# Forward substitution of two matrix sets at a time in a delta-rule attention kernel, with a separate early transpose of K

## Chip, cores and metric

The kernel runs on one core of a Trainium2 chip. The metric is device time in microseconds (us) of one execution. Engines: TensorE (PE; its weight loads are shown as PEld), VectorE (DVE), ScalarE (ACT), GpSimd (POOL) and SyncE (SP, which here only issues DMAs).

## What is computed

Inputs: q, k, v of shape (4, 8, 768, 48), beta (4, 8, 768), and the router and weights of 8 experts.

```python
k_n = k / (norm(k) + 1e-6); state = 0
for t in range(768):                       # for each of 4 x 8 heads
    y[t]  = q[t] @ state
    v_old = k_n[t] @ state
    state = state + beta[t] * outer(k_n[t], v[t] - v_old)
x = y, as 3072 tokens of 8 * 48 = 384
expert = argmax(x_n @ en.T / tau);  gate = softmax(...)[expert]
out[token] = gate * (relu(x[token] @ w1[expert]) @ w2[expert])   # 384 -> 1024 -> 384
```

All of it is in float32.

## The kernel before, in words

**Two halves.** The first half is the attention, in which each token also gets its expert. The second half (from line 1105 on) goes through the experts' token tiles of 128, some 11 us of TensorE each, with weights streamed by SP. Two expert tiles of expert 0 (`early_tile`) are already done at the end of the first half.

**Chunks, units, groups.** The sequence of 768 is cut into 12 chunks of 64 steps (`m`). A unit (`n`, 24 of them) is one chunk for two of the four batch entries, 16 heads at once; the units of one half of the batch follow each other through a state S, so two chains of units alternate. A group (`g`, 6 of them) is two chunks, or four units.

**What a unit does** (`unit`, line 626). Inside a chunk the sequential rule is a triangular system. A unit multiplies K with the state (`old`), subtracts from V (`rest`, VectorE), solves with the inverses of the two 32x32 blocks on the diagonal (`solve`, `fix`, `solve_again`, with copies out of PSUM by ScalarE between them), updates the state (`update`, `new_state` on VectorE), and adds the part from the state and the part inside the chunk to the output (`from_state`, `inside`). Then come the transposes of the output, the router's logits (`logits_out` on VectorE) and, for each four units, the routing.

**The inverses** are made ahead, a group at a time, by `prepare(g)` (line 422). K is loaded and normalised (the sums of squares, roots and the product `keys`), transposed on TensorE (`turned`, line 305) and evicted by ScalarE into `KQ`, whose other half holds q transposed. `gram_diag` makes the 32x32 Gram blocks on the diagonal: for a group 2 x 64 matmuls into one PSUM pair. A 32x32 transpose (`to_lanes`, line 546) puts them so that each of 128 partitions (lanes) holds one 32x32 matrix X. `lower` on GpSimd clears the upper part. Then VectorE substitutes column by column, lines 556 to 568: for j from 1 to 30 a product (line 561) and a subtraction (line 565) over (31 - j) * j elements. Each instruction needs the one ahead of it. That is 60 instructions a group, 360 in all. `from_lanes` (line 573) transposes back into `WT` (one buffer), and ScalarE spreads that into W (two instructions, `spread`), which all `solve` steps of the group's four units read. Some buffers (k, X, WT) lie in the space that later holds the first expert's weights.

**What sets the order.** Nothing is scheduled while the kernel runs: each engine executes its instructions in a fixed order. That order comes from `Plan` (line 29): each step is added with an engine, a cost, a due time (`key`, in units of `PERIOD` = 7.5 us) and what it reads and writes; `order` plays the steps through with these costs and always takes the ready step with the earliest due time. PSUM is four pairs of banks, which steps take and give back. So a change of a cost or of a due time can move any instruction.

SP issues the loads of k, q and v: each is cut into issues of 48 or 96 KB, 20 issues for a chunk (some of the first by other engines).

Of the kernel before, what the change touches and what calls it, by code (L numbers as in the profile page):

```python
# [11 lines left out]
ALU = mybir.AluOpType  # L12
# [4 lines left out]
C = 64  # L17
# [122 lines left out]
def kernel(  # L140
# [68 lines left out]
    def at(name, i):  # L209
        return name, i % len(rings[name])  # L210
# [9 lines left out]
    buffers("q", 2, [2, H, C])  # L220
    buffers("v", 3, [2, H, D])
    buffers("sq", 1, [2, H, D])
    buffers("K", 6, [2, H, C])
    buffers("KQ", 5, [2, NP, 2, 2 * C])
    buffers("rn", 2, [2, 2, NP, 2])
    buffers("rt", 2, [2, 2, NP, 2])
    quots = ac.tile([128, 2, 2, NP, 2], F32, name="quots")
    rings["X"], rings["WT"] = carved(2, [HC, HC], w2_flat), carved(3, [HC, HC], w2_flat)[2:]
    buffers("tmp", 2, [(HC // 2) * (HC // 2)])
    buffers("W", 2, [HC, C])  # L230
    buffers("Sx", 3, [H, C])
# [91 lines left out]

    flat_buffers("V", 3, 4 * NP * D)
    for name, n in (("S", 2), ("R", 2), ("Y", 2), ("U", 2), ("Z", 3)):
# [74 lines left out]
    def beta_refine(part):  # L400
# [4 lines left out]
    plan.add("POOL", 1.5, 0.2, -200.0, start_constants,  # L405
             writes=["ident", "half", "iotas"] + [("K", i) for i in range(6)] + [("q", i) for i in range(2)])

# [11 lines left out]
    def group_key(g):  # L419
        return 4 * g * PERIOD  # L420

    def prepare(g):
        ms = (2 * g, 2 * g + 1)
        t0 = group_key(g)
        for m in ms:
# [58 lines left out]
        for part in (slice(0, 1), slice(1, 2)) if g == 0 else (slice(0, 2),):  # L484
            xs = range(part.start, part.stop)
            those, roots_of = [at("rn", g) + (x,) for x in xs], [at("rt", g) + (x,) for x in xs]
            if g < 2:
                plan.add(*act(16 * len(xs)), t0 - 10 * PERIOD, roots_act(part), reads=those + ["half"], writes=roots_of)
            else:
                plan.add("POOL", 5.5, 0.2, t0 - 10 * PERIOD, roots(part), reads=those + ["half"], writes=roots_of)  # L490
            plan.add("DVE", 1.1 if g < 2 else 0.5, 0.2, t0 - 9.6 * PERIOD - (g == 0) * 30, scales(part), hold=g == 0,
                     reads=those, writes=roots_of + ["quots"])
            plan.add("DVE", 0.12 * len(xs), 0.2, t0 - 9.6 * PERIOD, scaled(part), hold=g == 0,
                     reads=[("sqb", 2 * g + x) for x in xs], writes=roots_of)

        def keys(m):
# [6 lines left out]

        def transposes(src, m, name):
            def step():
                turned(pair((name, m)), buf(src, m))
            return step

        def out_of_psum(m, name, cols):
            def step():  # L510
                act_copy(buf("KQ", m).rearrange("d i j y c -> d (i j y) c")[:, :, cols],
                         pair((name, m)).rearrange("d i (x c) -> d (i x) c", c=C))
            return step

        def gram_diag(m):
            def step_():
                p = pair(("diag", g))
                KQ = buf("KQ", m)
                for step in range(2 * NP):
                    for y in range(2):  # L520
                        for hf in range(2):
                            for jj in range(2):
                                n = 2 * NP - 1 - step if hf else step
                                rows = slice(jj * C, jj * C + D)
                                i, j, x = n // NP, n % NP, m % 2 * 2 * NP + n
                                r = (y ^ jj) * C + hf * HC
                                c, w = (0, C) if step < 2 * NP - 1 else (hf * HC, HC)
                                to = x * HC + c - hf * HC
                                mm(p[r:r + HC, jj, to:to + w], KQ[rows, i, j, y, hf * HC:(hf + 1) * HC], KQ[rows, i, j, y, c:c + w])
            return step_  # L530
        for m in ms:
            plan.add(*(dve(850) if m == 1 else pool(768)), t0 - 9.2 * PERIOD + (m % 2) * PERIOD, keys(m), hold=g == 0,
                     reads=[("k", m % 4, 0), ("k", m % 4, 1), at("rt", g) + (m % 2,)], writes=[at("K", m)])
            plan.add(*pe(8, 0.11), t0 - 8.6 * PERIOD + (m % 2) * PERIOD, transposes("K", m, "KT"), mode=2,
                     reads=[at("K", m), "ident"], take=("KT", m))
            plan.add(*act(1024), t0 - 8.4 * PERIOD + (m % 2) * PERIOD, out_of_psum(m, "KT", slice(0, C)),
                     reads=[("psum", ("KT", m))], writes=[at("KQ", m) + ("K",)])
        for m in ms:
            first = m % 2 == 0
            plan.add(*pe(64, 0.02), t0 - 7.2 * PERIOD, gram_diag(m), mode=1, reads=[at("KQ", m) + ("K",)],  # L540
                     writes=[("X_next", g % 2)] + ([] if first else [("psum", ("diag", g))]),
                     take=("diag", g) if first else None)
        X = buf("X", g)

        def to_lanes():
            nc.vector.transpose(X, pair(("diag", g)).rearrange("p jj (x c) -> p c jj x", c=HC))
        plan.add(*dve(1024), t0 - 6.5 * PERIOD, to_lanes, hold=g == 0, reads=[("psum", ("diag", g))],
                 writes=[at("X", g), ("X_next", g % 2)])

        def lower():  # L550
            nc.gpsimd.affine_select(out=X, in_=X, compare_op=ALU.is_ge, fill=0.0, base=-1,
                                    pattern=[[1, HC], [-1, HC]], channel_multiplier=0)
            nc.gpsimd.memset(X.rearrange("p a b -> p (a b)")[:, ::HC + 1], -1.0)
        plan.add("POOL", 1.2, 0.1, t0 - 6.4 * PERIOD, lower, writes=[at("X", g)])

        for j in range(1, HC - 1):
            rows = HC - 1 - j
            t = buf("tmp", j)[:, 0:rows * j].rearrange("p (a b) -> p a b", b=j)

            def product(j=j, rows=rows, t=t):  # L560
                nc.vector.tensor_tensor(t, X[:, j + 1:, j:j + 1].broadcast_to([128, rows, j]),  # L561
                                        X[:, j:j + 1, 0:j].broadcast_to([128, rows, j]), op=ALU.mult)

            def subtract(j=j, rows=rows, t=t):
                nc.vector.tensor_tensor(X[:, j + 1:, 0:j], X[:, j + 1:, 0:j], t, op=ALU.subtract)  # L565
            key = t0 - (6.0 - j * 4.0 / HC) * PERIOD
            plan.add("DVE", rows * j / 960 + 0.085, 0.13, key, product, reads=[at("X", g)], writes=[at("tmp", j)], hold=g == 0)
            plan.add("DVE", rows * j / 960 + 0.085, 0.13, key + 0.01, subtract, reads=[at("tmp", j)], writes=[at("X", g)], hold=g == 0)

        WT, W = buf("WT", g), buf("W", g)  # L570

        def from_lanes():
            nc.vector.transpose(WT, X)
        plan.add(*dve(1024), t0 - 1.9 * PERIOD, from_lanes, reads=[at("X", g)], writes=[at("WT", g), ("X_next", g % 2)])
        for b, name in enumerate(("nfirst", "nsecond")):
            def spread(b=b, name=name):
                act_copy(W[:, :, b * HC:(b + 1) * HC], WT.rearrange("p i x -> p x i"), K[name])
            plan.add(*act(1024, True), t0 - 1.8 * PERIOD, spread, reads=[at("WT", g), "masks"], writes=[at("W", g) + (b,)])

# [3 lines left out]
    def queries(m):  # L583
# [8 lines left out]

        def transposes():
            turned(pair(("QT", m)), buf("q", m))

        def evict():
            act_copy(buf("KQ", m).rearrange("d i j y c -> d (i j y) c")[:, :, C:],
                     pair(("QT", m)).rearrange("d i (x c) -> d (i x) c", c=C))
        plan.add(*pe(8, 0.11), t0 - 3.5 * PERIOD, transposes, mode=2, reads=[at("q", m) + (i,) for i in range(2)] + [("q", m % 2)] + ["ident"],
                 take=("QT", m))  # L600
        plan.add(*act(1024), t0 - 3.4 * PERIOD, evict, reads=[("psum", ("QT", m))], writes=[at("KQ", m) + ("Q",)])

# [406 lines left out]
    def early_tile(i, t0):  # L1009
# [47 lines left out]
        plan.add("PE", 0.4, 0.3, t0, transposes, mode=2, reads=[("xg", i), "ident"], take=("early_x", i))  # L1057
        plan.add(*act(384), t0 + 0.1, xT_out, reads=[("psum", ("early_x", i))], writes=["early_xT"])
        for f in range(NF):
            plan.add("PE", 0.7, 0.3, t0 + f, hidden(f), mode=2, reads=["early_xT", "w1_first"], take=("early_h", i, f))  # L1060
            plan.add(*act(128), t0 + f + 0.1, hidden_out(f), reads=[("psum", ("early_h", i, f))],
                     writes=[("early_hT", f)])
        for f in range(NF):
# [4 lines left out]

    prepare(0)
    constants()  # L1070
    for g in range(NG):
        for m in (2 * g, 2 * g + 1):
            queries(m)
            values(m)
        if g + 1 < NG:
            prepare(g + 1)
        if g == NG - 1:
# [218 lines left out]
```

## Time and profile before

| | us |
|---|---|
| median of 14 runs (lowest, highest) | 647.62 (643.64, 652.78) |
| the profiled execution, its time | 649.65 |
| its span in the profile | 647.9 |

| engine | busy, us | share of the span | instructions |
|---|---|---|---|
| PE | 551.6 | 85% | 9995 |
| DVE | 267.8 | 41% | 749 |
| ACT | 180.4 | 28% | 327 |
| POOL | 167.3 | 26% | 217 |

The profile also has the span in 40 slices with the busy share of each engine in tenths, and the clock that TensorE was granted (PEclk). Groups of instructions are shown as: line, engine, operation, output<-inputs, shapes, count | busy us, mean ns of one | idle time of the engine ahead of them, and whose end ended it. Rows in order of time have the start and the duration in us. Rows by stretch of time have, for each engine, the busy us and the number of instructions, then the granted clock and the DMA engines' share. A float32 matmul counts as two instructions.

### The profile page before, as it was taken

To read this page: it belongs to the slowest core of one execution; us is meant where nothing else is said; L and a number is where in the kernel's file an instruction comes from. 1 tells how busy PE (TensorE), PEld (TensorE's weight loads), DVE (VectorE), ACT (ScalarE), POOL (GpSimd) and SP (SyncE) were. 2 spreads that over 40 slices of the span, in tenths; PEclk is the share of its full clock that TensorE was granted. 3 is DMA by queue.
4 is the path that set the end of the run, shared out by engine and by line. 5 is a ranking of instruction groups with operands and counts; after the bars stand their busy time and mean duration, and the time that the engine had idled before them with its cause. 6 is when DMAs were issued, how large, how long until landed. Compare 5 with 4: busy or idle time off the path is not lost. (4 is left out here: it accounts for less than half of the span.)

```text
span 647.9 us, 22729 instructions
## 1 busy us (share of the span) xinstructions
PE 551.6 (85%) x9995; PEld 464.9 (72%) x9995; DVE 267.8 (41%) x749; ACT 180.4 (28%) x327; POOL 167.3 (26%) x217
## 2 busy tenths in 40 slices
PE   3563787778887888789997999999999999999991
PEld 3452676677776877678975787878788888878780
DVE  4898769669789687813232111111111111111100
ACT  2322625526527346354430111110101010101010
POOL 4434334254252131312221211212121212121100
PEclk9875669579879789968997999999999999999997
DMA  4444744533414221222013999999999999999500
GB/s 77 80 81 80 195 73 80 124 70 64 102 31 102 84 51 28 65 95 79 32 39 120 387 385 393 380 343 313 338 320 332 311 323 331 337 320 324 208 25 6
DMA packets 127911, 115.46 MB, mean 178 GB/s; under 512 B 83754, under 2 KB 113873, under 8 KB 127810
## 3 DMA queue, kind: packets, MB, share of 16 engines
q1 hardware_dynamic: 122242, 102.93, 51.6%
q0 software_dynamic: 4480, 10.85, 4.5%
q8 instruction: 80, 1.31, 0.8%
q10 hardware_dynamic: 1088, 0.20, 0.2%
q14 instruction: 21, 0.17, 0.1%
HBM read 102.02 MB, written 12.72 MB: 177 GB/s over the span
## 5 line engine op out<-in xcount | busy, mean ns | idle before, releaser
L1164 ACT ACTIVATE hT<-acc 128x512 f32<-128x512 f32 x52 | 31.1, 597 | 259.4 <-PE acc L1162 259.4
L1162 PEld LDWEIGHTS acc<-xTm,w 128*128 128x128 f32 x816 | 93.8, 192 | 4.5
L1162 PE MATMUL acc<-xTm,w 128*128 128x128 f32 x816 | 93.9, 275 | 0.0
L1169 PE MATMUL acc<-w,hT 128*128 128x384 f32 x272 | 90.5, 486 | 0.0
L1172 POOL DMA_INDIRECT out_dram<-y,ids x26 | 26.3, 1011 | 205.7 <-DVE y L1171 195.9
L1169 PEld LDWEIGHTS acc<-w,hT 128*128 128x128 f32 x272 | 50.4, 190 | 31.5
L565 DVE TENSOR_TENSOR w_first<-w_first,tmp 128x30 f32<-128x30 f32 (+9 forms) x180 | 69.6, 388 | 3.9
L1154 DVE COPY xTm<-acc 128x384 f32<-128x384 f32 x26 | 14.5, 558 | 134.4 <-PE acc L1153 134.4
L561 DVE TENSOR_TENSOR tmp<-w_first 128x30 f32<-128x30 f32 (+9 forms) x180 | 66.2, 370 | 4.1
L1171 DVE TENSOR_SCALAR y<-acc,xg 128x384 f32<-128x384 f32 x26 | 16.1, 618 | 125.0 <-PE acc L1169 125.0
L273 PE MATMUL psum_pair<-KQ 48*32 48x64 f32 (+2 forms) x2304 | 48.7, 271 | 18.7 <-issue 8.9
L273 PEld LDWEIGHTS psum_pair<-KQ 48*32 48x32 f32 (+1 forms) x2304 | 41.6, 137 | 24.1 <-issue 11.6
L1162 PEld LDWEIGHTS acc<-xTm,w_first 128*128 128x128 f32 x432 | 52.4, 201 | 3.2 <-DVE xTm L1154 1.0
L1162 PE MATMUL acc<-xTm,w_first 128*128 128x128 f32 x432 | 52.6, 284 | 0.8 <-DVE xTm L1154 0.8
L1169 PE MATMUL acc<-w_first,hT 128*128 128x384 f32 x144 | 47.9, 486 | 0.0
L273 PE MATMUL psum_pair<-S,KQ 48*64 48x64 f32 x1408 | 35.5, 249 | 10.3 <-issue 4.4
L273 PEld LDWEIGHTS psum_pair<-S,KQ 48*64 48x64 f32 x1408 | 30.7, 160 | 13.3 <-issue 5.9
L1169 PEld LDWEIGHTS acc<-w_first,hT 128*128 128x128 f32 x144 | 26.7, 190 | 16.7
L276 ACT ACTIVATE KQ<-psum_pair 128x1024 f32<-128x1024 f32 x24 | 24.5, 1023 | 42.8 <-PE psum_pair L309 33.7
L960 POOL DMA_INDIRECT idmap<-tokid,slots_i x24 | 24.2, 1008 | 42.6 <-DVE slots_i L936 13.2
L1137 POOL DMA_INDIRECT xg<-x_dram,ids x26 | 25.4, 975 | 37.7 <-DMA ids<-idmap 22.6
L615 POOL TENSOR_TENSOR V<-v,sqb 128x384 f32<-128x384 f32 x24 | 20.7, 866 | 49.8 <-DVE R L670 31.6
(183 smaller groups left out, 747.6 us busy)
## 6 DMA issues: line engine op xcount, KB each, us to landing
w<-in_moe_w_dram SPq DMA_DIRECT2D x34, 1536.0 KB
w_first<-in_moe_w_dram SPq DMA_DIRECT2D x16, 1536.0 KB
q<-in_q_dram SPq DMA_DIRECT2D x96, 48.0 KB
v<-in_v_dram SPq DMA_DIRECT2D x48, 96.0 KB
w_first<-in_k_dram SPq DMA_DIRECT2D x88, 48.0 KB
x_dram<-XC SPq DMA_DIRECT2D x5, 800.0 KB
idmap<-space SPq DMA_DIRECT2D x1, 2048.0 KB
w_first<-in_moe_w_dram SPq DMA_DIRECT2D x6, 256.0 KB
```

The costliest lines, as they stand in the source:

```text
L273: nc.tensor.matmul(out_, lhsT=lhsT, rhs=rhs, start=start, stop=True, skip_group_check=True)
L276: nc.scalar.activation(out_, in_, ACT.Copy, scale=scale)
L561: nc.vector.tensor_tensor(t, X[:, j + 1:, j:j + 1].broadcast_to([128, rows, j]), X[:, j:j + 1, 0:j].broadcast_to([128, rows, j]), op=ALU.mult)
L565: nc.vector.tensor_tensor(X[:, j + 1:, 0:j], X[:, j + 1:, 0:j], t, op=ALU.subtract)
L615: nc.gpsimd.tensor_tensor(buf("V", m)[:, i * 2 * NP * D:(i + 1) * 2 * NP * D].rearrange("p (jj j d) -> p jj j d", jj=2, d=D), buf("v", m)[ ...
L960: put = nc.gpsimd.indirect_dma_start(out=idmap[:, :], out_offset=bass.IndirectOffsetOnAxis(ap=slot_i[:, i:i + 1], axis=0), in_=K["tokid"][ ...
L1137: t.read = nc.gpsimd.indirect_dma_start(out=t.x, out_offset=None, in_=x_dram[:, :], in_offset=bass.IndirectOffsetOnAxis(ap=t.ids[:, 0:1], ...
L1162: nc.tensor.matmul(psH[:, i, :], lhsT=t.w1[:, j, (f + i) * 128:(f + i + 1) * 128], rhs=t.xT[:, j, :], start=(j == 0), stop=(j == KC - 1))
L1164: nc.scalar.activation(t.hT[:, f:f + 4, :], psH, ACT.Relu)
L1169: nc.tensor.matmul(psO, lhsT=t.hT[:, f, :], rhs=t.w2[:, f, :], start=(f == 0), stop=(f == NF - 1))
L1171: nc.vector.tensor_scalar_mul(y, psO, t.x[:, Dm:Dm + 1])
L1172: nc.gpsimd.indirect_dma_start(out=out[:, :], out_offset=bass.IndirectOffsetOnAxis(ap=t.ids[:, 1:2], axis=0), in_=y, in_offset=None, bound ...
```

## The change

Group 0 and group 1 are substituted alone as before, groups 2 and 3 together, and groups 4 and 5 together: two matrices a lane, in one instruction with one dimension more. So 240 substitution instructions stand where 360 stood, and 120 of them have twice the elements. The steps that prepare the two groups of a pair are due relative to the pair's first unit, brought forward by 3.5 periods (of 7.5 us) for its first group and by 2.5 for its second. K is transposed twice: early into a buffer `KT` of its own for the Gram on the diagonal, and again near its unit, into `KQ`. Ring sizes change: K 6 to 8, KQ 5 to 3, KT 2 new, v and V 3 to 2, tmp 2 to 1 (twice as large), W 2 to 3. The costs that the planner takes for the substitution (VectorE) and for `spread` (ScalarE) change as well.

The diff, cut to its core:

```diff
-    buffers("v", 3, [2, H, D])
+    buffers("v", 2, [2, H, D])
-    buffers("K", 6, [2, H, C])
-    buffers("KQ", 5, [2, NP, 2, 2 * C])
+    buffers("K", 8, [2, H, C])
+    buffers("KQ", 3, [2, NP, 2, 2 * C])
+    buffers("KT", 1, [2, NP, 2, C])
+    rings["KT"] += carved(1, [2 * NP, 2 * C], space[0])
-    rings["X"], rings["WT"] = carved(2, [HC, HC], w2_flat), carved(3, [HC, HC], w2_flat)[2:]
-    buffers("tmp", 2, [(HC // 2) * (HC // 2)])
-    buffers("W", 2, [HC, C])
+    X2, rings["WT"] = carved(1, [2, HC, HC], w2_flat)[0], carved(3, [HC, HC], w2_flat)[2:]
+    buffers("tmp", 1, [2 * (HC // 2) * (HC // 2)])
+    buffers("W", 3, [HC, C])
...
-    flat_buffers("V", 3, 4 * NP * D)
+    flat_buffers("V", 2, 4 * NP * D)
...
+    LANES = [[0], [1], [2, 3], [4, 5]]
+    lanes_of = {g: those for those in LANES for g in those}
     def prepare(g):
-        t0 = group_key(g)
+        those = lanes_of[g]
+        t0 = group_key(those[0]) - (3.5 - those.index(g)) * (len(those) > 1) * PERIOD
...
-            plan.add(*pe(8, 0.11), t0 - 8.6 * PERIOD + (m % 2) * PERIOD, transposes("K", m, "KT"), mode=2,
-                     reads=[at("K", m), "ident"], take=("KT", m))
-            plan.add(*act(1024), t0 - 8.4 * PERIOD + (m % 2) * PERIOD, out_of_psum(m, "KT", slice(0, C)),
-                     reads=[("psum", ("KT", m))], writes=[at("KQ", m) + ("K",)])
+            plan.add(*pe(8, 0.11), t0 - 8.6 * PERIOD + (m % 2) * PERIOD, early_transposes(m), mode=2,
+                     reads=[at("K", m), "ident"], take=("early_KT", m))
+            plan.add(*act(1024), t0 - 8.4 * PERIOD + (m % 2) * PERIOD, early_out(m),
+                     reads=[("psum", ("early_KT", m))], writes=[at("KT", m)])
...
+    def substitute(those):
+        two = len(those)
+        lo = those[0] % 2 if two == 1 else 0
+        X = X2[:, lo:lo + two]
+        names = [("X", lo + x) for x in range(two)]
+        t0, step = group_key(those[0]), (4.0 if two == 1 else 7.0) / HC * PERIOD
         for j in range(1, HC - 1):
             rows = HC - 1 - j
-            t = buf("tmp", j)[:, 0:rows * j].rearrange("p (a b) -> p a b", b=j)
+            n = two * rows * j
+            t = buf("tmp", j)[:, 0:n].rearrange("p (s a b) -> p s a b", s=two, b=j)
             def product(j=j, rows=rows, t=t):
-                nc.vector.tensor_tensor(t, X[:, j + 1:, j:j + 1].broadcast_to([128, rows, j]),
-                                        X[:, j:j + 1, 0:j].broadcast_to([128, rows, j]), op=ALU.mult)
+                nc.vector.tensor_tensor(t, X[:, :, j + 1:, j:j + 1].broadcast_to([128, two, rows, j]),
+                                        X[:, :, j:j + 1, 0:j].broadcast_to([128, two, rows, j]), op=ALU.mult)
             def subtract(j=j, rows=rows, t=t):
-                nc.vector.tensor_tensor(X[:, j + 1:, 0:j], X[:, j + 1:, 0:j], t, op=ALU.subtract)
-            key = t0 - (6.0 - j * 4.0 / HC) * PERIOD
-            plan.add("DVE", rows * j / 960 + 0.085, 0.13, key, product, reads=[at("X", g)], writes=[at("tmp", j)], hold=g == 0)
+                nc.vector.tensor_tensor(X[:, :, j + 1:, 0:j], X[:, :, j + 1:, 0:j], t, op=ALU.subtract)
+            key = t0 - 2.0 * PERIOD - (HC - j) * step
+            plan.add("DVE", n / 960 + 0.17, 0.04, key, product, reads=names, writes=[at("tmp", j)], hold=hold)
+    def out_of_lanes(g):
+        those = lanes_of[g]
+        half_of = those.index(g) if len(those) > 1 else g % 2
+        t0 = group_key(g) if half_of == 0 or len(those) == 1 else group_key(g) - 3.0 * PERIOD
...
-            plan.add(*act(1024, True), t0 - 1.8 * PERIOD, spread, reads=[at("WT", g), "masks"], writes=[at("W", g) + (b,)])
+            plan.add("ACT", 2.07, 0.16, t0 - 1.8 * PERIOD, spread, reads=[at("WT", g), "masks"], writes=[at("W", g) + (b,)])
...
+        for src, first, of in (("K", 0, [at("K", m)]), ("q", C, [at("q", m) + (i,) for i in range(2)] + [("q", m % 2)])):
+            def transposes(src=src):
+                turned(pair((src, "T", m)), buf(src, m))
+            def evict(src=src, first=first):
+                act_copy(buf("KQ", m).rearrange("d i j y c -> d (i j y) c")[:, :, first:first + C],
+                         pair((src, "T", m)).rearrange("d i (x c) -> d (i x) c", c=C))
+            plan.add(*pe(8, 0.11), t0 - 3.5 * PERIOD + first / C, transposes, mode=2, reads=of + ["ident"], take=(src, "T", m))
+            plan.add(*act(1024), t0 - 3.4 * PERIOD + first / C, evict, reads=[("psum", (src, "T", m))],
+                     writes=[at("KQ", m) + ("Q" if first else "K",)])
...
-    prepare(0)
+    def prepare_lanes(those):
+        for g in those:
+            prepare(g)
+        substitute(those)
+        for g in those:
+            if g != 5:
+                out_of_lanes(g)
+    prepare_lanes([0])
...
-        if g + 1 < NG:
-            prepare(g + 1)
+        if g + 1 < len(LANES):
+            prepare_lanes(LANES[g + 1])
+        if g == 3:
+            out_of_lanes(5)
```

## The prediction

> **What bounds the kernel now.** I read the page's 40 slices first, then busy times by stage, then VectorE's and TensorE's instructions in order of time. The slices show two halves:
>
> ```profile
> PE   3563787778887888789997999999999999999991
> DVE  4898769669789687813232111111111111111100
> PEclk9875669579879789968997999999999999999997
> ```
>
> A slice is 16.2 us. From slice 22 on TensorE is full with the experts; the change leaves them alone. VectorE is busy up to slice 17. I cut that half at the ends of the six transposes out of the lanes (L573, at 62.9, 112.6, 159.4, 198.3, 237.5 and 274.6 us, called W0 to W5) and asked for busy times:
>
> ```profile
> core 0: us, PE busy (x) PEld busy (x) DVE busy (x) ACT busy (x) POOL busy (x), PEclk, DMA share, GB/s
> 62.87:112.60 49.73, 39.02 (x1289) 34.40 (x1287) 39.67 (x102) 24.41 (x42) 20.57 (x20) 0.77 0.52 115
> ...
> 159.40:198.30 38.90, 30.72 (x1163) 28.05 (x1154) 32.33 (x96) 18.36 (x32) 16.44 (x18) 0.87 0.31 67
> 198.30:237.50 39.20, 31.91 (x1142) 28.98 (x1146) 31.52 (x92) 17.25 (x31) 11.78 (x16) 0.83 0.36 92
> 237.50:274.60 37.10, 30.16 (x1179) 27.00 (x1177) 30.55 (x94) 21.03 (x42) 7.87 (x11) 1.00 0.15 39
> 274.60:311.00 36.40, 33.28 (x1044) 30.34 (x1043) 9.54 (x31) 17.34 (x34) 6.37 (x9) 0.72 0.26 82
> 311.00:344.50 33.50, 33.48 (x463) 26.79 (x461) 10.96 (x61) 11.86 (x35) 7.43 (x11) 1.00 0.10 34
> ```
>
> Between W2 and W5 VectorE is busy 94.4 of 115.2 us; with the 0.035 us that the rows below leave between two of its 282 instructions it is 104, or 90%. TensorE is busy 92.8, or 81%. So VectorE leads with TensorE close behind. After W5 VectorE falls away and TensorE is busy 91%, then 100%, up to 344.5 us; the experts start 3.7 us later. The time to shorten is the 344.5 us, and it has two bounds in a row: VectorE to W5, TensorE after it.
>
> **What one substitution instruction costs.** Clean ones in order of time (start, duration):
>
> ```profile
> 42.17 0.40 DVE L561 TENSOR_TENSOR tmp<-w_first 128x234 f32<-128x234 f32 x1
> 42.61 0.41 DVE L565 TENSOR_TENSOR w_first<-w_first,tmp 128x234 f32<-128x234 f32 x1
> 43.05 0.41 DVE L561 TENSOR_TENSOR tmp<-w_first 128x238 f32<-128x238 f32 x1
> ...
> 60.71 0.19 DVE L561 TENSOR_TENSOR tmp<-w_first 128x30 f32<-128x30 f32 x1
> 60.93 0.19 DVE L565 TENSOR_TENSOR w_first<-w_first,tmp 128x30 f32<-128x30 f32 x1
> ```
>
> Start to start is 0.44 us at 234 elements and 0.22 at 30: 1.04 ns per element and a share of 0.19 us that is there at any size. The doubled instruction (60 to 480 elements) is not in this trace; its saving lies between nothing and 0.19. The nearest row is the keys' product, also two inputs in SBUF:
>
> ```profile
> L499 DVE TENSOR_TENSOR K<-w_first,rt 128x384 f32<-128x384 f32 x2 | 1.0, 554 | 0.0
> ```
>
> 384 x 1.04 = 400 ns leaves 154 of fixed share, so the share does not grow with size. I take 0.19.
>
> **Step 1: VectorE up to W5.** 360 instructions become 240, the elements stay: 120 x 0.19 = -22.8 us. The order of the changed kernel shows a second thing: W4 and W5 now leave the lanes together, when only 14 of 22 state updates have been issued; before it was 18. Four units' VectorE work moves behind W5: score masks 4 x 0.60, updates and right sides 8 x 0.50, logit copies 4 x 0.1, routing and other small ones 17 x 0.22, together 10.5 us. VectorE's work ahead of W5 falls by 33.3 us, but 10.5 of it is only moved.
>
> **Step 2: the start.** Ahead of the first Gram on the diagonal TensorE now also makes the late transposes of chunk 0, and ScalarE evicts them ahead of chunk 1's. The rows:
>
> ```profile
> L276 ACT ACTIVATE KQ<-psum_pair 128x1024 f32<-128x1024 f32 x24 | 24.5, 1023 | 42.8 <-PE psum_pair L309 33.7
> 19.81 1.97 PE L309 MATMUL psum_pair<-ident,K 128*128 128x128 f32 x8 [1.01 <-DVE K L499]
> ```
>
> That is 1.0 to 3.0 us; I take 2. Ahead of W0 VectorE also gets two more sums of squares (0.95 each) and ten small ones (2.5 us), already inside the sum of step 1. SP issues 16 more loads of K (0.63 us each, 10 us) ahead of the first queries, which then land near 43 us instead of 32. Unit 0 starts at 67 us now, so that alone hides. But on TensorE the transposes of chunk 6 stand directly ahead of unit 0's first solve, and chunk 6's keys wait on VectorE for roots that come 5.5 us after W0, then 1.7 us on GpSimd (L499, 2 x 0.85). Unit 0 starts some 9 us after W0 instead of 4.1, and the two units behind it wait too. VectorE has about 14 us of substitution to do meanwhile, so I charge 2 us (0 to 5).
>
> **Step 3: stalls.** VectorE's waits over 0.2 us between 64 us and W5 add to 35 us, nearly all for TensorE. Four fewer units of 18 pass there: 35 x 4/18 = -8. New ones: the second transpose out of a pair must wait until ScalarE has spread the first (one WT buffer; two spreads of 2.07 us against 1.2 us of other VectorE work): 3 us. The pair (4,5) begins right behind its second transpose into the lanes, so it waits for GpSimd's lower() (1.31 + 0.16): 2 us. With step 2 that is +7 (from 2, if most is covered, to 15, since between W1 and W3 TensorE must do six units and two diagonal Grams and is then as full as VectorE). The smaller rings I cost at nothing: SP waited for a free v buffer 5.5 us in all, once, and its queue is loose after 130 us; if a late v held V back, the unit's right side would wait, inside the upper end. W5 comes at 274.6 - 33.3 + 2 - 8 + 7 = 242.3 us.
>
> **Step 4: TensorE behind W5.** All of the old tail stays (69.9 us). Four units are added, and late K transposes of five chunks: 5 x 0.88 (start to start of the eight q transposes at full speed, 273.84 to 274.72) = 4.4 us. K was transposed once before and is now transposed twice. The other seven, and 12 evictions of 1.02 us on ScalarE (busy 56.6 of 115.2 us between W2 and W5), lie beside VectorE's work; uncovered they would cost 7 x 0.88 = 6 us. What a unit costs TensorE hangs on the granted clock:
>
> ```profile
> 283.00 1.16 PE L273 MATMUL psum_pair<-Y,Sx 64*64 64x64 f32 x32
> 295.97 0.69 PE L273 MATMUL psum_pair<-Y,Sx 64*64 64x64 f32 x32
> 279.00:291.00 12.00, 10.47 (x293) 9.60 (x287) 1.68 (x4) 5.30 (x11) 0.00 (x0) 0.55 0.15 49
> ```
>
> The same 32 passes take 1.16 us at the low clock and 0.69 at the full one. In the old tail units pass at 8.76 us (state updates at 282.27 and 308.55, three units) at a mean clock of 0.72. At a clock of 0.98 TensorE needs 6.7 us a unit (34.90 us busy from 230.5 to 274.6, 5.2 units), 7.05 at 95% busy. By the first, four units are 35 us: 242.3 + 69.9 + 35 + 4.4 = 351.6, or 7.1 later than now. By the second the old tail's own slow stretches go as well (about 20 us at the low clock, worth 8): 242.3 + 61.9 + 28.2 + 4.4 = 336.8, or 7.7 earlier. The mean clock from W0 to 311 us, by the rows, is near 0.8; I take a point between, weighted a little to the old tail, the only stretch without substitution: 347.4, **+2.9 us**.
>
> The Trainium skill, "TensorE: Matmul & The Clock Gate", section on the HAM clock gate, says that one busy window of about 3.4 us restores the full clock. By that rule the long tail would run at full speed, and the sum would be the -7.7. The row from 279 to 291 speaks against it: TensorE is busy 10.5 of 12 us, without a gap over 0.2 us after 281.0, and the granted clock is 0.55.
>
> **Sum.** The profiled execution took 649.65 us, 1.75 over its span and 2.0 over the median of the 14 runs (647.62). From the profile the sum is 652.5, from the median 650.5. I predict **651**.
>
> **Rivals.** About 0.3%, 2 us, is what a measurement of this kernel can tell from no change.
> - *Forecast, slightly slower (0.37)*: the tail at its old clock eats the saving; 650 to 659.
> - *Faster (0.28)*: the clock stays full while TensorE is dense, as from 237.5 to 274.6 (1.00). End 7.7 us earlier: about 640 from the median. It decides once the mean clock behind W5 is above 0.89 (between the two ends in a straight line, that is 2 us earlier than now). For it: VectorE's waits, which starve TensorE, are gone there. Against: the old tail.
> - *All of the saving arrives (0.07)*: VectorE is the bound throughout and TensorE takes the extra units in its gaps: -22.8, 625. Against: TensorE's 91% behind W5.
> - *Much slower (0.14)*: between W1 and W3 both engines are full and each waits in its own order for the other; step 3 takes 15 instead of 7 and the uncovered transposes 6: 651 + 14 = 665. It decides if W3 lies behind 180 us.
> - *No difference (0.14)*: gains and losses cancel within 2 us; 646 to 650. A doubled instruction that costs two single ones belongs to the slower cases: 22.8 us more.
>
> Faster by over 0.3%: 0.28 + 0.07 = 0.35. Within: 0.14 and the lower edge of the forecast, 0.17. Slower: 0.48. The range runs from 636 (the full clock and some fewer stalls) to 665 (the much slower case), leaving out the whole saving and the worst of the coupling.
>
> **What would show it.** Step 1: 240 substitution instructions, the 480-element ones near 0.66 us; VectorE's last transpose out of the lanes near 242 us, with eight state updates behind it. Step 2: first solve 8 to 10 us behind W0. Step 3: a wait of about 3 us ahead of the second transpose of a pair. Step 4: ten units behind W5 with TensorE over 90% busy, and their pace: near 8.8 us at a clock of 0.7, near 7.3 at 1.0. The prediction is wrong if the tail's clock is full, if doubled instructions cost double, or if the waits between W1 and W3 exceed 15 us.

## The result, and the profile after

The changed kernel takes 679.07 us (median of 10 runs, 674.14 to 685.52), the one before 647.07 beside it (47 runs): a ratio of **1.049**, interval 1.047 to 1.052. The profiled execution took 677.2 us, its span is 675.4, at a mean granted clock of 0.891. The profiles of two experiments below (the last pair alone, and less VectorE work) are of disturbed executions; their ratios leave such executions out. The runs were made on several chips, where the kernel before takes 644 to 659 us, so experiments are compared by their ratios. The two profiled executions are 27.6 us apart, the medians 32.

The slices after, VectorE and TensorE's clock around it:

```profile
PE   3545766878769887788999799999999999999992
...
DVE  5789794588727985122314011111111111111100
...
PEclk9759595587968996989899799999999999999996
```

A slice is 16.9 us. The first half now reaches into slice 23, and VectorE has valleys in slices 7, 8 and 12 (4, 5 and 2), where it stood at 9, 6 and 8 before. By stretches, cut at W0, W1, W3, W5, at 311 us and at 370.2, where TensorE ends the attention:

```profile
core 0: us, PE busy (x) PEld busy (x) DVE busy (x) ACT busy (x) POOL busy (x), PEclk, DMA share, GB/s
0.00:70.40 70.40, 32.80 (x832) 29.61 (x833) 55.01 (x144) 21.95 (x30) 34.81 (x72) 0.81 0.45 80
70.40:109.70 39.30, 26.23 (x823) 22.48 (x825) 30.69 (x82) 18.07 (x27) 12.05 (x10) 0.72 0.54 123
109.70:186.70 77.00, 61.67 (x2020) 55.65 (x2013) 53.68 (x110) 36.95 (x59) 28.57 (x26) 0.74 0.28 57
186.70:264.00 77.30, 61.90 (x2172) 54.98 (x2161) 53.06 (x119) 36.24 (x65) 20.77 (x27) 0.86 0.31 74
264.00:311.00 47.00, 38.79 (x1188) 35.23 (x1187) 11.58 (x37) 23.93 (x46) 10.46 (x14) 0.84 0.31 81
311.00:370.20 59.20, 56.18 (x1342) 47.29 (x1340) 18.32 (x85) 23.86 (x61) 12.77 (x18) 0.97 0.10 35
```

VectorE's busy time up to W5 fell: 192.4 us (the first four rows), against 216.1 before. But between W1 and W5 it is busy only 106.7 of 154.3 us, 69%; before, from W2 to W5, it was 82% (94.4 of 115.2). W5 stands at 264.0 us and not at 242.3. The experts' first transposes start at 374.8 us (before 348.2).

The instructions themselves do what they should. The two groups of substitution, 240 instructions for 360:

```profile
L574 DVE TENSOR_TENSOR tmp<-w_first 128x168 f32<-128x168 f32 (+28 forms) x120 | 59.4, 495 | 4.3 <-POOL w_first L557 1.4
L578 DVE TENSOR_TENSOR w_first<-w_first,tmp 128x168 f32<-128x168 f32 (+28 forms) x120 | 56.8, 473 | 3.0
```

Together 116.2 us busy against 135.8 (69.6 + 66.2): 120 instructions fewer save 19.6 us, 0.163 each.

What catches the eye first is that the substitution stands still, from 108.4 to 128.9 us and from 180.0 to 200.9; such a stretch is called a hole below and is measured to the next substitution instruction. The second hole, in order of time:

```profile
179.77 0.22 DVE L578 TENSOR_TENSOR w_first<-w_first,tmp 128x60 f32<-128x60 f32 x1
180.03 1.25 DVE L591 STREAM_TRANSPOSE w_first<-w_first 128x1024 f32<-128x1024 f32 x1
...
185.41 1.25 DVE L591 STREAM_TRANSPOSE w_first<-w_first 128x1024 f32<-128x1024 f32 x1 [3.10 <-ACT W L279]
...
189.24 1.25 DVE L552 STREAM_TRANSPOSE w_first<-psum_pair 128x1024 f32<-128x1024 f32 x1 [2.58 <-PE psum_pair L276]
...
198.30 1.25 DVE L552 STREAM_TRANSPOSE w_first<-psum_pair 128x1024 f32<-128x1024 f32 x1 [7.37 <-issue]
...
200.92 0.26 DVE L574 TENSOR_TENSOR tmp<-w_first 128x60 f32<-128x60 f32 x1 [1.37 <-POOL w_first L557]
```

The lanes hold two matrices. Before, one group was substituted in one half while the next group's Gram went into the other. A pair fills both halves. So its two transposes out (L591) come first, the next pair's two Grams (TensorE) and transposes in (L552) follow one by one, and only then does the next subtraction start. VectorE's waits over 0.2 us between 64 us and W5 add to 50.2 us; they were 34.8. That made the first theory.

### The profile page after: what moved, and what is told of

The parts are those of the page before. It is cut to its first block, busy times and chain, and to the rows that moved or that the text cites. A ratio compares the mean times of both kernels' runs of the same rounds, so it can differ in the third digit from the quotient of the medians.

```text
span 675.4 us, 22842 instructions
## 1 busy us (share of the span) xinstructions
PE 563.1 (83%) x10091; PEld 474.7 (70%) x10091; DVE 253.8 (38%) x629; ACT 192.0 (28%) x339; POOL 172.0 (25%) x218
## 5 line engine op out<-in xcount | busy, mean ns | idle before, releaser
L1182 DVE COPY xTm<-acc 128x384 f32<-128x384 f32 x26 | 14.5, 558 | 135.9 <-PE acc L1181 135.9
L574 DVE TENSOR_TENSOR tmp<-w_first 128x168 f32<-128x168 f32 (+28 forms) x120 | 59.4, 495 | 4.3 <-POOL w_first L557 1.4
L578 DVE TENSOR_TENSOR w_first<-w_first,tmp 128x168 f32<-128x168 f32 (+28 forms) x120 | 56.8, 473 | 3.0
L312 PE MATMUL psum_pair<-ident,K 128*128 128x128 f32 x192 | 34.1, 341 | 7.3 <-DVE w_first L552 4.1
L276 PE MATMUL psum_pair<-S,KQ 48*64 48x64 f32 x1408 | 34.8, 246 | 6.0 <-DVE S L738 4.0
L634 POOL TENSOR_TENSOR V<-v,sqb 128x384 f32<-128x384 f32 x24 | 22.5, 948 | 60.4 <-DVE R L689 34.8
L312 PEld LDWEIGHTS psum_pair<-ident,K 128*128 128x128 f32 x192 | 29.0, 180 | 9.6 <-DVE w_first L552 4.4
L312 PE MATMUL psum_pair<-ident,q 128*128 128x128 f32 x96 | 16.5, 325 | 19.1 <-DMA q<-in_q_dram 17.4
```

Of the source, the lines that this page charges most:

```text
L276: nc.tensor.matmul(out_, lhsT=lhsT, rhs=rhs, start=start, stop=True, skip_group_check=True)
L312: nc.tensor.transpose(p[:, i, j * 128:(j + 1) * 128], two, ident)
L574: nc.vector.tensor_tensor(t, X[:, :, j + 1:, j:j + 1].broadcast_to([128, two, rows, j]), X[:, :, j:j + 1, 0:j].broadcast_to([128, two, row ...
L578: nc.vector.tensor_tensor(X[:, :, j + 1:, 0:j], X[:, :, j + 1:, 0:j], t, op=ALU.subtract)
L634: nc.gpsimd.tensor_tensor(buf("V", m)[:, i * 2 * NP * D:(i + 1) * 2 * NP * D].rearrange("p (jj j d) -> p jj j d", jj=2, d=D), buf("v", m)[ ...
```

## The experiments

The theories, as they are named in the expectations. **A**: the holes cost the time. **B**: K's second transposition and its evictions do. **C**: the smaller rings or the planner's new costs do. **D**, after the first four runs: TensorE's own work bounds the attention, so what VectorE saves comes to little. **E**, after four more: TensorE is the bound from the first units on, and the pair's preparation, planned ahead of those units, makes them late.

One measure recurs below: the first *state update*, the first `S<-S,psum_pair` on VectorE (L738; L719 before). The chains of units hang on these; there are 20, and the first is unit 2's. Times are from the profiled executions. e1, e4, e5 and e6 ran on the chip where the kernel before takes 658.6 us, the others where it takes 644 to 648. Behind the experts' start all profiles have 298 to 303 us, so the times of these four stand some 10 us higher by the experts' start than on the other chips (an estimate), and only the ratio compares them with the rest.

| run | ratio (interval) | W0 | first update | W5 | experts start |
|---|---|---|---|---|---|
| before | 1 | 62.9 | 101.9 | 274.6 | 348.2 |
| after | 1.049 (1.047, 1.052) | 70.4 | 115.8 | 264.0 | 374.8 |
| e1 singles | 1.016 (1.008, 1.024) | 64.4 | 102.0 | 280.3 | 362.9 |
| e4 costs | 1.002 (0.998, 1.005) | 62.6 | 95.7 | 276.8 | 353.5 |
| e5 K twice | 1.011 (1.001, 1.021) | 62.9 | 103.9 | 278.8 | 360.7 |
| e6 three places | 1.029 (1.013, 1.045) | 69.7 | 119.7 | 263.0 | 371.7 |
| e7 three places, first pair | 1.036 (1.029, 1.043) | 69.8 | 123.5 | 291.7 | 365.0 |
| e8 last pair | 1.023 (1.017, 1.029) | 63.8 | 101.4 | 269.4 | 368.8 |
| e9 first pair | 1.039 (1.031, 1.046) | 70.0 | 115.4 | 295.8 | 366.5 |
| e10 Grams early | 1.060 (1.054, 1.065) | 71.0 | 133.5 | 273.9 | 383.0 |
| e11 pairs due later | 1.055 (1.047, 1.063) | 67.0 | 108.6 | 281.3 | 376.9 |
| e12 singles due early | 1.036 (1.028, 1.044) | 69.9 | 114.9 | 270.2 | 365.0 |
| e13 less VectorE work | 0.998 (0.995, 1.002) | 62.2 | 100.6 | 266.2 | 349.4 |
| e14 first pair due later | 1.034 (1.029, 1.039) | 65.9 | 110.4 | 271.7 | 370.9 |

**e1, every group alone**

```diff
-    LANES = [[0], [1], [2, 3], [4, 5]]
+    LANES = [[g] for g in range(NG)]
```

> The changed kernel, but every eight units alone again (two halves of the lane space in turn, as before the change); the separate transposition of K for the diagonal Gram, the late one, the smaller rings and the planner's new costs stay. Theory A (a pair fills the whole lane space, so the next Grams can only begin when the pair has left, and substitution stands still for some 20 us twice): the two holes go, no stretch of more than 5 us without a subtract between groups, W5 back at about 275 to 282, and the time 648 to 660, at least 19 below the changed kernel's 679. Rival B (the second transposition of K and its eviction): 672 to 682, hardly better than the changed kernel. Rival C (rings and costs): also 672 to 682, with the stretches of waiting still there.

Measured: ratio 1.016, and no hole of 20 us (the longest is 9.5 us, at 234.4). B and C alone are out as the whole cause: two thirds of the loss come with the pairs (with their early due times too, which e1 also takes back). But 1.6% stays without any pair.

**e4, the planner's costs alone** (kernel before)

```diff
-            plan.add("DVE", rows * j / 960 + 0.085, 0.13, ...)
+            plan.add("DVE", rows * j / 960 + 0.17, 0.04, ...)
```

> The kernel before with nothing but the planner's two new cost figures (substitution n/960+0.17 and 0.04, W's spreads 2.07 and 0.16). Theory A: the order of the engines' work moves a little, the time stays within 5 us of 647. Rival C (the new figures reorder the work for the worse): 660 or more. Rival B says nothing of it beyond 647.

Measured: 1.002, no difference. That half of C is out. In its profile the second chain gets its first state at 88.8 us (77.3 before; 78.5 in e5, on the same chip as e4), yet the first update comes earlier, at 95.7: a late first state of one chain need not cost.

**e5, K transposed twice** (kernel before)

```diff
+        plan.add(*pe(8, 0.11), t0 - 3.5 * PERIOD, again, mode=2, reads=[at("K", m), "ident"], take=("again", m))
+        plan.add(*act(1024), t0 - 3.4 * PERIOD, again_out, ...)
```

> The kernel before plus a second transposition of each K (8 matmuls and one eviction on ScalarE, twelve times; result unused, output unchanged). Theory A with the record's step 4: five of the twelve lie in TensorE's tail at 0.88 each, so plus 4, and 0 to 8 in all: 647 to 655. Rival B: the second K transposes and the 12 evictions carry most of the loss, 665 or more.

Measured: 1.011, or 7 us (0.5 to 13.5), at the upper end of the first expectation (0 to 8). B is a part of what the singles lose. TensorE's transposes of K take 30.7 us here and 16.2 before, so 14.5 us more of its work cost about half of that (by the interval, from next to nothing to nearly all).

**e6, three places in the lanes**

```diff
-    X2, rings["WT"] = carved(1, [2, HC, HC], w2_flat)[0], carved(3, [HC, HC], w2_flat)[2:]
+    X3 = carved(1, [3, HC, HC], w2_flat)[0]
+    buffers("WT", 1, [HC, HC])
...
+    PLACE = {0: 1, 1: 0, 2: 1, 3: 2, 4: 0, 5: 1}
```

> The changed kernel with three places in the lane space instead of two (W's transposed source in a buffer of its own; a row of squares in bfloat16 and two narrower scratch tiles pay for the room). The pair of groups 2 and 3 uses places 1 and 2 and can have place 2 filled early, and place 1 from the end of group 0; the pair 4 and 5 uses 0 and 1, so one of its two Grams can go early and the other still waits for group 2 to leave. Theory A: the first hole (108.2 to 128.9 in the changed kernel) shrinks to under 6 us, the second (179.8 to 200.9) by about half, so 20 to 30 us off the changed kernel: 650 to 660. Rivals B and C: no more than 5 us off, 674 to 680.

Measured: 1.029 (1.013 to 1.045), 2 points or 13 us better than the change, where A expected 20 to 30 and B and C at most 5. The first hole is gone: the pair's first product starts at 113.28, ahead of group 1's transpose out. The second grew to 29.5 us (172.6 to 202.1), since chunk 11's keys wait until 190.9 us for a K buffer that TensorE had not yet released. And the first state update came 4 us later still, at 119.7. VectorE's waits up to W5 were 50.0 us, as many as in the change. The hole was closed on VectorE and opened elsewhere; that raised D.

**e7, e8, e9, one pair at a time**

```diff
-    LANES = [[0], [1], [2, 3], [4, 5]]
+    LANES = [[0], [1], [2, 3], [4], [5]]    # e9; e7 on top of e6's three places
+    LANES = [[0], [1], [2], [3], [4, 5]]    # e8
```

> Three places in the lane space as in the run before, but only groups 2 and 3 are a pair; groups 4 and 5 go alone. No group waits for a place of its own any more. Theory A (the holes of the substitution and the late start cost the time): no hole over 10 us, W5 some 8 to 15 us ahead of the run with single groups, and a ratio to the kernel before of 0.99 to 1.01, against 1.016 with singles and 1.029 with three places and two pairs. Rival D, which that last run raised (TensorE's own work from W0 on, 245 to 254 us, is the bound, so VectorE's savings come to little): 1.01 to 1.02, with TensorE idle 40 us or more between W0 and the end of attention only if VectorE still starves it.

> The changed kernel with groups 0 to 3 alone and only 4 and 5 as a pair, two places. Theory A: one hole of about 20 us ahead of the pair, eight units behind W5, TensorE's part behind W5 about 105 us; ratio 1.03 to 1.04, between the singles (1.016) and the change (1.049). Rival D: the ratio is near 1.02, since TensorE has units to do while VectorE waits.

> The changed kernel with only groups 2 and 3 as a pair and 4 and 5 alone, two places. Theory A: a hole of about 20 us ahead of the pair and a second, smaller one ahead of group 4 (whose Gram waits until group 2 has left); TensorE's part behind W5 back at 80 us; ratio 1.025 to 1.04. Rival D: 1.015 to 1.02.

Measured: 1.036, 1.023 and 1.039. The last pair costs little over the singles (their intervals overlap) though its eight units stand behind W5 and a hole of 16.4 us stands ahead of it. The first pair costs 2 points, with a third place or without. By the expectations, e8 is D's, e9 is A's by its ratio, and e7 is slower than both allowed. What sets e7 and e9 apart from e8 and e1 in the table is the first state update: 123.5 and 115.4 us against 101.4 and 102.0. Holes do so too, so these runs alone don't decide: e7, which was to have none, has one of 45.1 us (170.8 to 215.9), and e9 has three of 19.5, 27.3 and 18.1. But TensorE does not wait for W once behind the first solve in e7, and 1.8 us in e9.

**e10, the Grams not held back**

```diff
-                     writes=[("X_next", half_of)] + ...
+                     writes=([] if len(those) > 1 else [("X_next", half_of)]) + ...
```

> The changed kernel with one thing undone: the planner no longer holds a pair's diagonal Grams back until the lanes are free (only the move into the lanes still waits), so they can run early and wait in PSUM. Theory A: the first hole shrinks from 20.5 us to about 5 (out of the lanes, into them, lower part), the second from 20.9 to about 10 (two spreads of W lie between the two ways out); W5 15 to 25 us earlier than 264, ratio 1.018 to 1.035 against 1.049. If the holes had another cause (K's second transposition, rings), they stay near 20 us and the ratio at 1.045 or more.

Measured: 1.060, the slowest of all; A failed here. The first hole did shrink, to 13.8 us, but the second grew to 45.6, and the first state update slipped to 133.5. In TensorE's order two more sets of K transposes and two more Gram halves now stand between the first chain's first solve (76.3) and the second's (110.1), and ahead of the second TensorE waits until VectorE has moved a Gram into the lanes:

```profile
107.98 1.13 PE L276 MATMUL psum_pair<-Z,M 64*64 64x64 f32 x32 [11.46 <-DVE w_first L552]
```

**e12, singles with the pairs' due times** (on e1)

```diff
-        t0 = group_key(those[0]) - (3.5 - those.index(g)) * (len(those) > 1) * PERIOD
+        t0 = {2: 4.5, 3: 5.5, 4: 12.5, 5: 13.5}.get(g, 4.0 * g) * PERIOD
```

> The run with single groups (ratio 1.016), but the preparation of groups 2 to 5 is due as early as the change has it for its pairs. No pair and no hole of a pair. Theory E: the first state update slips from 102.0 to 112 us or later, and the ratio rises to 1.03 to 1.045. Theory A: nothing changes, 1.01 to 1.02.

Measured: 1.036, first update at 114.9: both as E had it. No pair is in this kernel, its longest hole is 10.4 us, and TensorE never waits for W behind the first solve. The due times alone cost 2 points (1.016 to 1.036; by the two intervals, 1 to 3). The singles (e1), the first solves of the two chains on TensorE, and the second chain's first state and the first update on VectorE:

```profile
71.26 0.69 PE L276 MATMUL psum_pair<-V,W 64*64 64x64 f32 x32
72.45 0.69 PE L276 MATMUL psum_pair<-V,W 64*64 64x64 f32 x32 [0.49 <-ACT space L279]
79.39 0.55 DVE L740 COPY S<-psum_pair 128x384 f32<-128x384 f32 x1
102.00 0.54 DVE L738 TENSOR_TENSOR S<-S,psum_pair 128x384 f32<-128x384 f32 x1
```

The same with early due times (e12):

```profile
80.92 1.13 PE L276 MATMUL psum_pair<-V,W 64*64 64x64 f32 x32
93.03 1.13 PE L276 MATMUL psum_pair<-V,W 64*64 64x64 f32 x32
99.88 0.56 DVE L740 COPY S<-psum_pair 128x384 f32<-128x384 f32 x1 [0.61 <-PE psum_pair L276]
114.86 0.54 DVE L738 TENSOR_TENSOR S<-S,psum_pair 128x384 f32<-128x384 f32 x1
```

The first solve is 9.7 us later, behind group 2's Gram and chunk 6's transposes, and the second chain's first solve comes 12 us behind it instead of 1.2: the two chains no longer start side by side. Up to there TensorE's order is the changed kernel's, instruction by instruction.

**e11 and e14, the pairs due later**

```diff
-        t0 = group_key(those[0]) - (3.5 - those.index(g)) * (len(those) > 1) * PERIOD
+        t0 = group_key(those[0]) + those.index(g) * PERIOD                            # e11: both pairs
+        t0 = group_key(those[0]) - (3.5 * (g > 3) - those.index(g)) * PERIOD          # e14: the first pair
```

> The changed kernel, pairs and all, but a pair's preparation (loads, roots, K's transposes, diagonal Grams) is due 3.5 unit periods later than the change put it: the first group's at its own time, the second's one period behind. Theory E (what the runs so far point to: the pair's preparation, planned ahead of the first units, delays the first state update, at 101.9 us in the kernel before, 115.8 in the changed one, 119.7 to 133.5 in the runs that let it go earlier still; from there on TensorE takes 238 to 257 us whatever VectorE does): first update back at 102 to 108, the holes in the substitution as long as before or longer, and yet a ratio of 1.02 to 1.04. Theory A (the holes are the cost): the same holes or longer ones, ratio 1.05 or more.

> The changed kernel with only the pair of groups 2 and 3 due 3.5 periods later; the pair of 4 and 5 is due as the change has it, so that the second hole stays as it was. Theory E with the run before it (both pairs due later: first state update at 108.6 us, second hole 53 us, ratio 1.055): first update at 107 to 111, second hole about 21 us, ratio 1.03 to 1.045, better than the change's 1.049. Theory A: the longer first hole costs more than the start gives, ratio 1.05 to 1.06.

Measured: 1.055 and 1.034. In e11 the first update came back to 108.6, but the second hole grew from 20.9 to 52.8 us and W5 slipped to 281.3: A's ratio was right, and E's too low. e14 has the earlier start with a hole of 31.9 us (176.1 to 208.0; 21 was expected) and is 1.5 points faster than the change. What a late pair costs TensorE can be seen: it waits for the pair's first W, in e11

```profile
181.61 1.13 PE L276 MATMUL psum_pair<-R,W 64*64 64x64 f32 x32 [11.46 <-ACT W L279]
```

and 6.87 us in e14. Behind e11's hole of 52.8 us it waits for W only 1.06 us more (at 280.1), so the hole itself is not shown to be the cost. A pair has no good due time among those tried: early it delays the first units, late TensorE waits for it.

**e13, 23 us less for VectorE** (kernel before)

```diff
         for j in range(1, HC - 1):
+            if g > 1 and j % 4 == 1:
+                continue
```

> The kernel before, every group alone, with 64 of the 240 substitution instructions of groups 2 to 5 left out (each fourth step, so the solution matrices of these groups are incomplete and the tokens that the experts get differ): 64 x 0.19 us and 4992 elements x 1.04 ns x 2, 22 us of VectorE's work, as much as the pairs were to save, with no pair, no second K transposition and no new due time. The record's view (VectorE leads up to W5 and units pass behind it): W5 15 to 22 us earlier and the experts 8 to 20 us earlier, ratio 0.97 to 0.99. Theory E (TensorE with its chain of units is the bound from the first state update on, VectorE runs ahead of it): W5 earlier, but the experts start within 5 us of before, ratio 0.992 to 1.008.

Measured: 0.998 (0.995 to 1.002): the saving brings nothing. E's expectation held and the record's did not. Between W0 and W5 VectorE was busy 145.2 us, against 168.4 before, and its waits over 0.2 us grew from 34.8 to 51.6; W5 moved by 8.4 us only. Two late waits of e13 (a transpose in, and the subtraction behind it), and its last two state updates:

```profile
231.92 1.25 DVE L546 STREAM_TRANSPOSE w_first<-psum_pair 128x1024 f32<-128x1024 f32 x1 [4.60 <-PE psum_pair L273]
234.55 0.22 DVE L563 TENSOR_TENSOR tmp<-w_first 128x58 f32<-128x58 f32 x1 [1.38 <-POOL w_first L551]
...
299.27 0.56 DVE L721 TENSOR_TENSOR S<-S,psum_pair 128x384 f32<-128x384 f32 x1 [0.87 <-ACT Y L276]
309.84 0.55 DVE L721 TENSOR_TENSOR S<-S,psum_pair 128x384 f32<-128x384 f32 x1 [1.15 <-PE psum_pair L273]
```

The last two state updates of the kernel before:

```profile
299.38 0.56 DVE L719 TENSOR_TENSOR S<-S,psum_pair 128x384 f32<-128x384 f32 x1 [0.97 <-PE psum_pair L273]
308.55 0.56 DVE L719 TENSOR_TENSOR S<-S,psum_pair 128x384 f32<-128x384 f32 x1 [1.15 <-PE psum_pair L273]
```

These two pass at the same times within 1.3 us; of the other 18 updates, 15 lie within 2.1 us of before and three (262 to 282 us) come 2.6 to 5.5 us later. VectorE finished groups 3 and 4 early and waited for TensorE's next Gram (a hole of 19.7 us, 214.9 to 234.6).

## Why the prediction was wrong, point by point

**What bounds the kernel** is the step that failed. I read that VectorE is 90% occupied and TensorE 81% and made VectorE the leader up to W5. e13 shows that it isn't: with 23 us less to do it waits more. The share counted instructions that had slack. The profile of the kernel before shows this without any experiment. The second spread of W5 ends at 280.2 us, and TensorE begins the first solve that reads it (unit 20's) at 293.9:

```profile
278.18 2.06 ACT L276 ACTIVATE W<-w_first,nsecond 128x1024 f32<-128x1024 f32 x1
...
293.92 0.69 PE L273 MATMUL psum_pair<-R,W 64*64 64x64 f32 x32
```

Counted in the same way, unit 4 waited 1.9 us for W1, and W2 to W5 were ready 1.9, 9.9, 9.6 and 13.7 us ahead of their first solve. In the changed kernel W1 to W5 were ready 26.0, 12.7, 40.5, 13.5 and 45.5 us ahead, the second of them here:

```profile
183.32 2.06 ACT L279 ACTIVATE W<-w_first,nsecond 128x1024 f32<-128x1024 f32 x1
...
198.11 1.14 PE L276 MATMUL psum_pair<-R,W 64*64 64x64 f32 x32
```

So no solve of the changed kernel waited for the substitution, holes or not. (The planner orders TensorE's work by times that it expects; what it put ahead of a solve because it expected W late would not show here as a wait.) That TensorE, with the chain of units through it, is the bound instead is argued: e13 and these rows take VectorE out, TensorE is busy 85% of the stretch behind the first update, and e5's 14.5 us of more work for it cost about 7 (0.5 to 13.5). No run took work from TensorE.

Counted on TensorE, the loss of the profiled executions is plain. Before, cut at the first state update and at the end of attention:

```profile
0.00:101.85 101.85, 60.69 (x1845) 52.75 (x1845) 76.80 (x202) 35.00 (x55) 42.22 (x79) 0.75 0.48 96
101.85:344.50 242.65, 205.43 (x6408) 182.47 (x6408) 159.82 (x495) 114.34 (x221) 72.47 (x85) 0.85 0.29 69
```

After, the same cuts:

```profile
0.00:115.77 115.77, 62.34 (x1757) 55.02 (x1761) 87.33 (x229) 44.76 (x61) 51.20 (x83) 0.76 0.48 95
115.77:370.20 254.43, 215.23 (x6604) 190.22 (x6596) 135.00 (x345) 116.24 (x226) 68.24 (x82) 0.85 0.25 61
```

The second number is the stretch, the third TensorE's busy time. Its idle time ahead of the first update grew from 41.2 to 53.4 us (+12.3), its busy time there by 1.7; behind it the busy time grew by 9.8 and the idle time by 2.0. Together 25.7 us, from 344.5 to 370.2. Of the busy time, K's transposes take 17.9 us more (34.1 for 16.2), and the rest of the work took 6.4 less. None of VectorE's 19.6 us comes back in this sum.

**Step 1, VectorE's work**: right in the price of an instruction. A subtraction of 480 elements takes 0.654 us (0.66 said; the products, some of them beside GpSimd, 0.80), 0.163 us busy and 0.035 of gap were saved per instruction (0.19 said), and four state updates moved behind W5 (12 pass ahead of it instead of 16). The whole came out smaller: up to W5 VectorE's busy time fell by 23.7 us, with the gaps some 28, where 33.3 were said.

**Step 2, the start**: the delay seen, its reason right in part, the price wrong. I said that W0 would come 2 us later, and that unit 0 would start some 9 us behind W0 because chunk 6's transposes stand ahead of it and wait for their keys; and I charged 2 us for that, "VectorE has about 14 us of substitution to do meanwhile". The kernel before:

```profile
61.64 1.23 DVE L573 STREAM_TRANSPOSE w_first<-w_first 128x1024 f32<-128x1024 f32 x1
67.00 1.99 PE L273 MATMUL psum_pair<-V,W 64*64 64x64 f32 x64 [3.25 <-ACT W L276]
77.28 0.56 DVE L721 COPY S<-psum_pair 128x384 f32<-128x384 f32 x1 [0.79 <-PE psum_pair L273]
```

The kernel after:

```profile
69.21 1.23 DVE L591 STREAM_TRANSPOSE w_first<-w_first 128x1024 f32<-128x1024 f32 x1
71.25 1.90 PE L276 MATMUL psum_pair<-KT 48*32 48x64 f32 x125
...
80.09 1.97 PE L312 MATMUL psum_pair<-ident,K 128*128 128x128 f32 x8
...
81.99 1.13 PE L276 MATMUL psum_pair<-V,W 64*64 64x64 f32 x32
...
99.46 0.55 DVE L740 COPY S<-psum_pair 128x384 f32<-128x384 f32 x1
```

W0 is 7.5 us later, the first solve another 7.4 (11.6 behind W0), and the second chain's first state is 22 us later. The keys were not what the transposes waited for: GpSimd had them at 77.2, and TensorE was busy until 80.1 with group 2's Gram, which I had not counted there, and with another unit's scores. If TensorE is the bound, this is loss and not cover. e12, which has these due times and no pair, puts it at 2 points of ratio, about 13 us.

**Step 3, stalls**: -8 for four fewer units and +7 new made about 34 us of waits; measured 50.2. The waits that I named are there (3.10 us for `WT` at 185.41, 1.37 for `lower` at 200.92; 3 and 2 said). I missed that the next pair's Grams can't be placed until the pair has left. These 16 us are most of what W5 (264.0) lost against the 242.3 said; the rest is about what step 1 fell short. But W5 is not where the time went: e12, without a hole over 11 us, is 3.6% slower than before, and in the changed kernel no solve waits for W. No run closed both holes of the pairs: e6 and e10 shortened the first and lengthened the second.

**Step 4, the tail**: from W5 to the end 106.2 us against 105.1, which is luck: the clock was 0.84 and then 0.97, on average better than the old tail's (0.91 against 0.85), and yet seven units took 68.3 us (state updates from 267.5 to 335.8), 9.8 each against 7.3 to 8.8. TensorE was idle 8.2 of the first 47 us. I also took seven late transposes of K and twelve evictions at nothing, as lying beside VectorE's work; e5 measures all twelve at 7 us (0.5 to 13.5), with 4.4 said.

**The rivals**: the much slower one came nearest. Its condition, W3 behind 180 us, was met (186.7). Of its mechanism one half is there: TensorE's fixed order holds solves back behind a pair's preparation, ahead of the first update above all. The other half is not: between W1 and W3 VectorE was busy 70% and TensorE 80%, not both full. Its price of 14 us was less than half of the 32 measured. The sign of the faster case, a mean clock above 0.89 behind W5, came too (0.91), and the time was longer all the same.

**What stays open.** From e12 (1.036) to the change (1.049) some 9 us are left. The last pair may be part (e8, not told apart from the singles), and so may the lump of four Gram halves and their transposes that a pair puts between two units (state updates at 181.2 and 210.5 us, 29 us apart where 10 is usual, TensorE busy 21.5 of it). No run isolated these. TensorE's idle time behind the first update has 21.9 us for which the profile shows no cause, against 14.2 before. The first update doesn't set the time alone either: e11 has it at 108.6 and a ratio of 1.055, e7 at 123.5 and 1.036. The smaller rings were not tried alone; with K's second transposition and the new costs they are inside e1's 1.6%.

## What to carry to other kernels

When two engines are both above 80%, the busier one need not be the bound: look how long its results lie ready before their first reader starts, and leave out some of its work to see whether the time moves, before building a change that saves it. Batching two independent pieces makes both pieces' preparation due at once: price what that work pushes back on the other engine, first of all the work that opens the long chain, and price a late start in full unless its engine is shown to have slack. A pair that takes both halves of a double buffer has given up the double buffer.

## What the runs showed of the hardware

VectorE's substitution instructions took more than twice their time beside GpSimd. In the changed kernel, VectorE and GpSimd in order of time:

```profile
46.19 5.74 POOL L509 TENSOR_TENSOR K<-w_first,rt 128x384 f32<-128x384 f32 x6 [0.41 <-DVE rt L488]
47.48 0.92 DVE L574 TENSOR_TENSOR tmp<-w_first 128x234 f32<-128x234 f32 x1
48.43 0.91 DVE L578 TENSOR_TENSOR w_first<-w_first,tmp 128x234 f32<-128x234 f32 x1
51.89 3.85 POOL L634 TENSOR_TENSOR V<-v,sqb 128x384 f32<-128x384 f32 x4
57.36 0.40 DVE L574 TENSOR_TENSOR tmp<-w_first 128x228 f32<-128x228 f32 x1
```

While GpSimd multiplies K and V (six in 5.74 us, 0.96 each), an instruction of 234 elements takes 0.92 us; the clean row that the prediction shows has 0.40. Ten in a row between 46.5 and 56.0 us are slowed so, about 5 us ahead of W0. The kernel before has some 3 us of the same ahead of its W0 (four instructions between 33.6 and 37.0 us at 0.78 to 0.82, one at 44.4 at 1.02), so this is some 2 us of W0's 7.5 (an estimate). The Trainium skill, "SBUF — State Buffer", section "Who interferes with whom", says that a VectorE instruction with two inputs in SBUF contends with a GpSimd instruction that reads SBUF, and calls the shared ports an exclusive lock. The rows fit: VectorE starts one instruction per GpSimd instruction, 0.95 us apart.
